# When two weight loads and four transposing loads may start, in a one-core forward and backward pass of an attention and feed-forward block

## The chip, the cores and the metric

The kernel runs on one core of one Trainium2 chip. The metric is the time of one execution on the device in microseconds (us), and lower is better. A core has TensorE (PE in the profile) for matrix products, VectorE (DVE), ScalarE (ACT) and GpSimd (POOL) for the rest, and SyncE (SP), which here only issues transfers. POOL issues transfers too, through a queue of its own, and a few come from ACT. An engine works through its own list of instructions strictly in the order in which the program lists them: an instruction that has to wait holds back all that stand behind it on that engine, transfers to be issued included.

## The reference, cut to what matters

The reference returns the output of a block and the gradients of seven inputs for a given `grad_out`. Sequence length is 2048, width 512, 32 heads of 16, feed-forward width 1792, all bf16.

```
def _A_ref(x, wqkv, wo):            # attention over 8 positions back, in steps of 2
    q, k, v = split(x @ wqkv)
    logits = einsum(q, k gathered at pos - 2*w, w = 0..7) * scale
    attn = softmax(logits)
    return einsum(attn, v gathered) @ wo
def _B_ref(x, w1, b1, w2, b2):
    return gelu(x @ w1 + b1) @ w2 + b2
h  = x + _A_ref(layernorm(x), wqkv, wo)
h2 = h + _B_ref(layernorm(h), w1, b1, w2, b2)
```

`jax.vjp` of `h2` gives the gradients of x, wqkv, wo, w1, b1, w2 and b2.

## The kernel before, in words

The 2048 tokens are worked in four chunks of 512 (`c` = 0 to 3). The forward pass has these steps for each chunk, each a function.

- `f_ln1` and `f_qkv` (lines 348 to 377): layer norm, the projection to q, k or v, and the writing of the result to a buffer in DRAM (`q_r`, `k_r`, `v_r`) with four transfers.
- `f_attn` (line 417): products of q and k on DVE (`pa`), their sums over a head on PE (`lg`), the softmax, whose `Exp` on ACT is line 436, and the writing of the weights to `at_r` by four POOL transfers (line 442). The mark `("e", c, i)` is set on the `Exp` of half `i` of chunk `c`.
- `f_o` (line 444): the weights are read back by SP (`a`, line 300), v is read by SP in four parts (`v`, line 282), DVE multiplies the two (`pbo`, line 330, eight instructions per chunk), PE sums (`pso`), and ACT copies the result to `otm` (line 451). The mark `("o", c, qd)` is set on the copy of part `qd`. The result is written to DRAM by POOL (line 452) and transposed on PE and ACT to `oT`.
- `f_h` (line 457): product with `wo` on PE (`psh`, line 463), residual on DVE (line 464), the second layer norm (statistics on DVE at lines 259 to 261, a power on POOL at line 263, its application at line 265), writing to DRAM by POOL (line 467), transposing to `ln2T`.
- `f_ffn1` (line 497): first feed-forward product with `w1` on PE (`psf`, line 506), gelu on ACT and DVE, and three POOL transfers for each of seven steps (`x_d`, `s_d`, `g_d`, line 526).
- `f_ffn2` (line 529): product with `w2` (line 535).

Lines 553 to 634 write these calls out in an order that mixes the chunks. That order is not the order on the engines: the framework's scheduler lists each engine's instructions by priority and by the time at which it reckons them ready. So a transfer that is written early but depends on something late can stand behind others in the queue. `gate(ins, key)` (line 111) makes an instruction depend on the one that set a mark.

`w1` and `w2` are loads of 1792 KB each, both issued by POOL (lines 584 and 587). Their buffers are shared with earlier data: `w1` takes over `early1` (x of chunks 1 and 2 and a transposed layer norm), `w2` takes over `early` (k and q of chunk 1, read by the `pa` products of `f_attn(1)`). `w1` is first read by `f_ffn1(0)`, `w2` by `f_ffn2(0)`.

The backward pass ends with three weighted sums per chunk (`b_sum(c, sel)`, line 847). For `sel` 1, the last of the three, each of four parts is two DVE products (`pb`), a PE sum (`pss`) and an ACT copy (line 863) into `gt`. The mark `("s", c, sel)` is overwritten by each part, so after the call it stands for the fourth. Then `b_gx` (line 878) needs the three results of a chunk transposed (`gT`), multiplies them with `wqkvT` on PE (`psy`, line 892) and goes through the backward layer norm (`ln_bwd`, line 643). For chunks 0 and 1 all transposing is done by PE. For chunks 2 and 3 `b_gT` (line 868) has POOL write the results of `sel` 2 and 0 to DRAM (`gq_d`, line 875) and SP load them back transposed (`gTo`, line 876); `sel` 1 is transposed by PE. All four transposing loads are gated on `("s", 3, 1)`. For chunks 2 and 3 `psy` takes the operands in the order `sel` 1, 2, 0. Products for the gradient of wqkv (`psq`, line 929) are mixed in between.

## Time and profile before

| | |
|---|---|
| median of 6 runs | 714.42 us |
| lowest to highest | 712.17 to 720.34 us |
| the profiled execution: its time | 712.17 us |
| its span, first to last instruction | 709.9 us |
| mean granted TensorE clock | 0.955 |
| PE busy | 623.0 us (88%) |
| DVE busy | 556.5 us (78%) |
| ACT busy | 395.3 us (56%) |
| transfers | 163.57 MB, mean 230 GB/s |

The profiled execution is one of the six. It stands 2.25 us below their median, and 2.27 us of its time lie outside the span. In a timeline a line gives the start and the length of a group of instructions, the engine, the line of the kernel, the operation with output and inputs, and in brackets how long the engine was idle before it and what ended that. POOLq and SPq are the queues in which POOL and SP issue transfers; a line there shows the issuing, not the landing. In a table by stretches (windows) each engine's busy time is followed by the number of its instructions, then come the granted TensorE clock as a share of full speed, the mean busy share of the 16 DMA engines, and what they moved in GB/s.

### The profile page before, as it was taken

What the parts mean: (1) busy time and instruction counts of PE and PEld (TensorE: products, weight loads), DVE (VectorE), ACT (ScalarE), POOL (GpSimd) and SP (SyncE); (2) the same over time, 40 slices, a digit from 0 to 9 for tenths busy, and PEclk for the clock granted to TensorE, in tenths of its full rate; (3) what the DMA queues carried; (4) which work ended last, traced back from release to release, by engine and by line L of the source; (5) the groups of instructions that cost most, each with busy time, mean ns of one, the idle gap of its engine ahead of it and who ended that gap; (6) DMA issues with size and microseconds to landing.
All of it is one profiled execution on the core that took longest, in us unless ns stands there. A gap on an engine that the chain in (4) does not pass through costs nothing. (4 is left out here: it accounts for less than half of the span.)

```text
span 709.9 us, 10264 instructions
## 1 busy us (share of the span) xinstructions
PE 623.0 (88%) x3614; PEld 264.6 (37%) x3682; DVE 556.5 (78%) x919; ACT 395.3 (56%) x548; POOL 210.0 (30%) x318
## 2 busy tenths in 40 slices
PE   1898668779789499999999999998999999999985
PEld 0333222234243134444444444443533333334432
DVE  6467958778973859975988788477899999999754
ACT  5654425877957739845867687552131135357543
POOL 4324323534533433452452433313200410001000
PEclk9999887969989789999999999999999999999999
DMA  8597798664789659666775985849799999986642
GB/s 236 149 270 224 197 372 277 233 254 155 253 296 232 222 156 209 200 200 256 198 213 103 182 210 142 256 117 245 287 355 378 312 340 302 347 294 202 172 105 67
DMA packets 103221, 163.57 MB, mean 230 GB/s; under 512 B 60961, under 2 KB 69250, under 8 KB 103170
## 3 DMA queue, kind: packets, MB, share of 16 engines
q1 hardware_dynamic: 73824, 78.40, 40.4%
q0 software_dynamic: 24720, 80.07, 34.7%
q10 hardware_dynamic: 4626, 4.46, 1.9%
q8 instruction: 28, 0.46, 0.3%
q14 instruction: 23, 0.19, 0.1%
HBM read 90.97 MB, written 56.71 MB: 208 GB/s over the span
## 5 line engine op out<-in xcount | busy, mean ns | idle before, releaser
L330 DVE TENSOR_TENSOR pb<-ba,r 128x2048 bf16<-128x2048 bf16 x96 | 111.5, 1220 | 0.6 <-PE ptq L274 0.3
L506 PE MATMUL psf<-ln2T,w 128*128 128x512 bf16 x218 | 57.7, 396 | 12.6 <-ACT u L508 11.9
L535 PE MATMUL ps<-w,g 128*128 128x512 bf16 x216 | 55.2, 379 | 0.3
L788 PE MATMUL psw<-h1tm,ln2a 128*128 128x512 bf16 (+1 forms) x249 | 53.4, 353 | 0.5 <-issue 0.3
L667 PE MATMUL psw<-gout,gtm 128*128 128x512 bf16 x202 | 50.4, 379 | 2.8 <-DMA gtm<-g_d 1.5
L719 PE MATMUL psx<-w1T,gh 128*128 128x512 bf16 x211 | 49.8, 379 | 0.3
L330 DVE TENSOR_TENSOR pbo<-a,v 128x2048 bf16<-128x2048 bf16 x32 | 38.2, 1218 | 14.1 <-DMA a<-at_r 9.6
L372 ACT CAST qkv<-psq 128x512 bf16<-128x512 f32 x48 | 27.6, 585 | 32.2 <-PE psq L370 32.0
L697 PE MATMUL psg<-goutT,w2T 128*128 128x512 bf16 x161 | 41.2, 379 | 0.4
L508 ACT ACTIVATE u<-psf,b1c 128x512 bf16<-128x512 f32 x56 | 36.0, 681 | 7.9 <-PE psf L506 4.8
L506 PEld LDWEIGHTS <-w 128*128 128x128 bf16 x224 | 20.9, 100 | 41.5 <-issue 24.0
L518 ACT ACTIVATE s<-z 128x1024 bf16<-128x1024 bf16 x28 | 29.6, 1059 | 11.5 <-DVE z L516 7.2
L710 POOL DMA_DIRECT2D h1tm_d<-th x27 | 20.6, 762 | 50.2 <-ACT th L708 36.3
L313 DVE TENSOR_TENSOR pag<-go,bv 128x2048 bf16<-128x2048 bf16 x24 | 28.6, 1220 | 8.5 <-DMA go<-go_r 4.4
L863 ACT ACTIVATE gt<-pss 128x512 bf16<-128x512 f32 x32 | 19.1, 597 | 28.5 <-PE pss L336 28.5
L708 ACT COPY th<-pth 128x1024 bf16<-128x1024 bf16 x27 | 27.0, 1000 | 11.5 <-PE pth L706 10.9
L788 PEld LDWEIGHTS <-ln2a 128*128 128x128 bf16 x256 | 22.6, 98 | 27.7 <-issue 10.2
L689 ACT ACTIVATE by<-bu 128x1024 bf16<-128x1024 bf16 x21 | 22.2, 1057 | 19.2 <-DVE gb1p L699 16.4
L892 PE MATMUL psy<-wqkvT,gT 128*128 128x512 bf16 x121 | 30.9, 379 | 0.7 <-DVE lua L653 0.2
L929 PE MATMUL psq<-gt,ln1a 128*128 128x512 bf16 x123 | 31.1, 380 | 0.3 <-issue 0.2
L526 POOL DMA_DIRECT2D g_d<-g x28 | 20.6, 734 | 36.3 <-DVE g L520 34.5
L336 PE MATMUL pss<-pb,sel 128*32 128x512 bf16 x384 | 29.5, 384 | 0.6 <-DVE pb L330 0.2
(221 smaller groups left out, 1361.1 us busy)
## 6 DMA issues: line engine op xcount, KB each, us to landing
v<-v_r SPq DMA_DIRECT2D x16, 576.0 KB, 6.9
r<-go_r SPq DMA_DIRECT2D x16, 576.0 KB, 7.6
r<-k_r SPq DMA_DIRECT2D x16, 576.0 KB, 6.9
r<-q_r SPq DMA_DIRECT2D x16, 576.0 KB, 5.6
g_d<-g POOLq DMA_DIRECT2D x28, 256.0 KB, 4.2
h1tm_d<-th POOLq DMA_DIRECT2D x27, 256.0 KB, 4.5
h1tm<-h1tm_d POOLq DMA_DIRECT2D x3, 2048.0 KB, 12.1
x_d<-u POOLq DMA_DIRECT2D x21, 256.0 KB, 5.5
```

The source lines that it names most:

```text
L330: last = nc.vector.tensor_tensor(out=pr[:], in0=_ap(a_ap, [a_ap.ap[0], [2 * H, CJ], [0, Q4], [1, H]], off=wh * H + (4 * H * wh if sg else 0)),
L336: mm = nc.tensor.matmul(ps[PR * n:PR * n + PR, :], lhsT=sel4[:], rhs=prs[wh][:, TC * n:TC * n + TC, :, :].rearrange("p j d h -> p (j d h)" ...
L506: nc.tensor.matmul(ps[:], lhsT=w1[0][:, dc, ft * P:(ft + 1) * P], rhs=ln2T[:, dc, :], start=(dc == 0), stop=(dc == DC - 1))
L508: nc.scalar.activation(out=u[:, i, :], in_=ps[:], func=ACT.Identity, bias=b1c[:, ft:ft + 1], scale=1.0)
L518: nc.scalar.activation(out=s[:], in_=z[:], func=ACT.Sigmoid, scale=2.0 * GC)
L535: nc.tensor.matmul(ps[:], lhsT=gs[ft // 2][:, ft % 2, j * P:(j + 1) * P], rhs=w2[0][:, ft, :], start=(ft == 0), stop=False)
L667: nc.tensor.matmul(ps[:], lhsT=gtm[:, t, :], rhs=gout[t // TC][:, t % TC, :], start=(t == 0), stop=(t == NT - 1))
L697: nc.tensor.matmul(ps[:], lhsT=w2T[:, dc, ft * P:(ft + 1) * P], rhs=gT[:, dc, :], start=(dc == 0), stop=(dc == DC - 1))
L719: nc.tensor.matmul(ps[:], lhsT=t1s[ft // 2][:, ft % 2, j * P:(j + 1) * P], rhs=w1T[:, ft, :], start=(ft == 0), stop=(ft == FT - 1))
L788: nc.tensor.matmul(ps[:, 0:nf * P], lhsT=ln2a[:, t // TC, t % TC, dc * P:(dc + 1) * P], rhs=tmx[:, t, 0:nf * P], start=(t == 0), stop=(t = ...
L892: nc.tensor.matmul(ps[:], lhsT=gT[sel][:, g, j * P:(j + 1) * P], rhs=wqkvT[:, sel * G + g, :], start=(n == 0), stop=(n == NJ - 1))
L929: nc.tensor.matmul(ps[:], lhsT=ln1a[t // TC][:, t % TC, dc * P:(dc + 1) * P], rhs=gts[sel, t // TC][:, t % TC, :], start=(t == 0), stop=(t ...
```

## The change

Three things are edited, and no instruction is added or taken out.

1. The load of `w1` is written right after `f_attn(1)` instead of after `f_o(0)`, and it waits for the `Exp` of the first half of chunk 1 instead of the first `otm` copy of chunk 0.
2. The load of `w2` is written after `f_o(1)`, behind `f_qkv(2, 2)` and `f_ffn1(0)`, instead of after `f_h(0)`. It waits for the first `otm` copy of chunk 1 instead of the `Exp` of the first half of chunk 1. The wait for its buffer (the `pa` products of chunk 1) is there in both.
3. Each part of `b_sum` also gets a mark of its own for `sel` 0 and 1. The two transposing loads of chunk 2 are gated on the first part of the last sum (`("s", 3, 1, 0)`), the two of chunk 3 on its third part (`("s", 3, 1, 2)`); before, all four waited for its fourth.

```
     f_attn(1)
+    w1.append(fl.tile([P, DC, F], BF16, name="w1", tag="w1", bufs=1))
+    gate(pq.dma_start(out=w1[0][:], in_=B_w1.rearrange("(dc p) f -> p dc f", p=P)), ("e", 1, 0))
     f_o(0)
-    w1.append(fl.tile([P, DC, F], BF16, name="w1", tag="w1", bufs=1))
-    gate(pq.dma_start(out=w1[0][:], in_=B_w1.rearrange("(dc p) f -> p dc f", p=P)), ("o", 0, 0))
     f_h(0)
-    w2.append(fb.tile([P, FT, D], BF16, name="w2", tag="w2", bufs=1))
-    gate(pq.dma_start(out=w2[0][:], in_=B_w2.rearrange("(ft p) d -> p ft d", p=P)), ("e", 1, 0))
     f_qkv(2, 2)
     mix(f_ffn1(0), none)
     f_o(1)
+    w2.append(fb.tile([P, FT, D], BF16, name="w2", tag="w2", bufs=1))
+    gate(pq.dma_start(out=w2[0][:], in_=B_w2.rearrange("(ft p) d -> p ft d", p=P)), ("o", 1, 0))
     f_h(1)
...
-                mark["s", c, sel] = nc.scalar.activation(out=o_ap, in_=i_ap, func=ACT.Copy, scale=scale)
+                mark["s", c, sel] = mark["s", c, sel, qd] = nc.scalar.activation(out=o_ap, in_=i_ap, func=ACT.Copy, scale=scale)
...
-            gate(sync.dma_start_transpose(out=gTs[sel, c], in_=d_t[:, :]), ("s", 3, 1))
+            gate(sync.dma_start_transpose(out=gTs[sel, c], in_=d_t[:, :]), ("s", 3, 1, 2 * (c - 2)))
```

## The prediction

> **What bounds the kernel now.** I read the page's busy shares and slices first, then the table by stretches around the two weight loads, then the timelines of POOL, SP and DVE there, and last the timelines of the end.

> ```profile
> PE 623.0 (88%) x3614; PEld 264.6 (37%) x3682; DVE 556.5 (78%) x919; ACT 395.3 (56%) x548; POOL 210.0 (30%) x318
> ...
> PE   1898668779789499999999999998999999999985
> ```

> PE is nearly full in the backward pass (slices of 17.7 us, from the 15th on) and has its holes in the forward pass. So a stall of PE in the backward pass costs its own length, and a forward wait costs what it delays the chain between DVE, PE and ACT. The loads of w1 and w2 lie in the sixth slice:

> ```profile
> 80.00:90.00 10.00, 6.82 (x54) 2.62 (x52) 9.86 (x11) 6.30 (x11) 4.72 (x8) 0.98 0.74 204
> 90.00:100.00 10.00, 8.69 (x38) 3.06 (x37) 5.17 (x11) 1.60 (x2) 2.78 (x5) 0.68 1.03 352
> 100.00:110.00 10.00, 3.85 (x23) 1.04 (x21) 6.11 (x11) 2.83 (x5) 2.69 (x4) 0.83 1.02 412
> 110.00:120.00 10.00, 8.68 (x46) 3.59 (x43) 7.25 (x9) 5.26 (x7) 2.81 (x5) 0.66 0.65 210
> ```

> From 90 to 110 us the DMA engines are full (1.03, 1.02), while PE is busy for only 3.85 us of the second ten. POOL's queue, then SP's, then DVE:

> ```profile
> 85.28 2.17 POOL L179 DMA_DIRECT2D at_r<-attn  x4 [10.77 <-DVE attn L440]
> 87.44 1.13 POOL L587 DMA_DIRECT2D w<-in_B_w_dram  x1
> ...
> 93.46 0.76 POOL L584 DMA_DIRECT2D w<-in_B_w_dram  x1
> ```

> ```profile
> 70.12 2.39 SPq L300 DMA_DIRECT2D a<-at_r  x4
> ...
> 93.75 4.53 SPq L300 DMA_DIRECT2D a<-at_r  x4
> 98.33 1.89 SPq L282 DMA_DIRECT2D v<-v_r  x3
> ```

> ```profile
> 100.50 0.17 DVE L260 BATCH_NORM_AGGREGATE mvb<-stb 128x2 f32<-128x6 f32 x1
> 104.21 1.23 DVE L330 TENSOR_TENSOR pbo<-a,v 128x2048 bf16<-128x2048 bf16 x1 [3.54 <-DMA a<-at_r]
> 105.35 0.17 DVE L260 BATCH_NORM_AGGREGATE mvb<-stb 128x2 f32<-128x6 f32 x1
> 105.44 1.19 DVE L330 TENSOR_TENSOR pbo<-a,v 128x2048 bf16<-128x2048 bf16 x1
> 106.55 0.16 DVE L261 TENSOR_SCALAR veb<-mvb 128x4 f32<-128x4 f32 x1
> 107.06 2.36 DVE L330 TENSOR_TENSOR pbo<-a,v 128x2048 bf16<-128x2048 bf16 x2 [0.35 <-DMA v<-v_r]
> 109.34 1.38 DVE L265 TENSOR_SCALAR ln<-h,mvb,rstd 128x512 bf16<-128x512 bf16 x4
> ```

> The weights of chunk 1 are written at 85.28 and w2 (3.5 MB with w1) starts right behind them. SP can read them back only from 93.75, its four issues take 4.53 us where those of chunk 0 took 2.39, and DVE stands still for 3.54 us. Behind that pbo, in DVE's order, is the layer norm of chunk 0, for which the first psf at 114.47 waits. At the other end:

> ```profile
> 668.28 4.94 SPq L876 DMA_TRANSPOSE gTo<-gq_d  x2
> ```

> ```profile
> 674.07 1.03 PE L892 MATMUL psy<-wqkvT,gTo 128*128 128x512 bf16 x4
> 677.15 1.04 PE L892 MATMUL psy<-wqkvT,gTo 128*128 128x512 bf16 x4 [2.05 <-DMA gTo<-gq_d]
> ```

> The copy that opens the gate ends at 668.26 and the first transposing load starts at 668.28: the gate is the last wait. PE, otherwise full here, loses 2.05 us.

> **The change part by part.** Nothing is added; three waits move. I take each against the profiled execution (712.17 us, span 709.9).

> w1 goes earlier. Its new gate, the Exp at 72.89, ends at 73.5; POOL is then issuing the v writes until 74.5 and afterwards idle until 85.28 (10.77 us). So the issue (0.76 to 1.13 us) costs POOL nothing, and what is behind it in that queue, the at_r writes, comes 10 us later. The load landed in 11.6 and 15.4 us beside the other, so from 75 it is there by about 90, against a first use at 114.47. Its buffer is free: the last psq product on it ends by 66.4. From 78.4 to 81.7 nothing moves at all, so there is room. It can only hurt the weights of chunk 0, issued 70.12 to 72.5 and used at 78.56. Their landing has a median of 4.9 us and a maximum of 6.9; with the maximum they come at 79.4, 0.85 late. Bounds 0 and +0.85; I take +0.2, since they mostly land before w1 moves.

> w2 goes later. Its gate, the copy at 107.83, moves forward with the rest to about 104. I expect the issue after POOL's power for the layer norm (106.80 now), because the veb that releases that power precedes the copy (106.55 and 107.83). Were it ahead, the power would wait for the copy's end (108.41 now) and for an issue of 1.13 us: 108.41 + 1.13 - 106.80 = 2.7 us more; the bounds are 0 and +2.7, and I take 0. Behind it in POOL's queue are v writes and the ln2 write, read by nothing until later chunks, and then the x_d writes from 118.81; u has three buffers, and an x_d write that lands at the page's median of 5.5 us instead of the 3.3 measured there would hold the fourth u back by at most 2.2. I take 0, as 111 to 118 are nearly idle for DMA. w2 is first used at 155.36, so 13.5 us from 108 leaves over 30 us to spare.

> What goes: the at_r writes end at 87.45. For chunk 0 SP started 3.47 us after their end (66.65 to 70.12); so 90.9, four issues 2.39, the last landing 4.9 after its start, 97.6. That is 3 us before DVE gets to the pbo at 100.67. The v loads follow at 93.3 and land 6.6 later, at 99.9 to 101.2, before they are used. Both waits go: 3.54 + 0.35 = 3.89. They cannot give more, because DVE is then in its own work, and the 4.67 us of idle before 95.33 wait for psh, a chain of pso, copy, transpose and product without a transfer. What is late next is PE: its v projection ends at 103.03 and pso can follow at once.

> The clock. PE stands still 3.66 us before 106.69, and from 108 to 116 the granted clock is 0.50. The 15 transposes ptb took 0.93 + 1.01 where 8 take 0.61 elsewhere, 0.75 more; seven psf took 1.49 + 1.21 where seven take 1.69 at 118.81, 1.0 more. So between 0 and 1.75 us come on top; I take 1.0, since the clock was also low (0.68) from 90 to 100, where no gap of PE exceeds 1 us. [...]

> [...]

> The transposing loads. Chunk 2's new gate is the copy at 656.18; its writes to gq_d, issued at 654.70 and 655.45, land in 4.6 and 5.4 us, at 660.9. Two loads take 4.94 us to issue and land 5.2 to 6.6 after their start, so by about 670; the first use is at 674.07. Chunk 3's gate opens at 664.6; its loads follow, are issued by 670.4, and are needed from about 682. In SP's queue the gx writes of chunk 1, ready at 670.7, are behind them; the last r load (651.90) is ahead. The stretch 663 to 668 has no transfers at all. The 2.05 us go (bounds 0 and 2.26, with the 0.21 at 681.64); behind them PE finds all operands, and the ring of two psy buffers moves up with it.

> Sum: -3.89 - 1.0 + 0.2 - 2.05 = -6.74 us, that is 705.4 in an execution like the profiled one. That one lies 2.25 below the median, so 714.42 - 6.74 = 707.7.

> **The rivals.**
> 1. The forward gain is given back before 260 us. For it: later holes, such as DVE's 6.03 us for the weights of chunk 3 at 229.72 and ACT's 2.40 for an s_d write at 147.46. Against it: these follow from work before them and move with it. Only the end gains: 712.4.
> 2. Only the forward part gains, because the loads at the end start early but land late among the gq_d writes: 714.42 - 4.69 = 709.7. Against it: 4 us of slack.
> 3. Nothing changes, each wait being replaced by one of its length: 714.4.
> 4. Slower: w2 sits in POOL's queue behind the stores of f_ffn1(0), since it is now written behind them. First use 155.36, less 4.7 gained, is 150.7; the landing takes 13.5. Break-even is a landing 6.7 late, at 157.4, so an issue at 143.9, or 148.6 on the clock before: behind the s_d store at 148.81 or a later one it decides. Behind the last g_d store (157.0, less 4.7, is 152.3) it lands at 165.8, 15.1 late; 707.7 + 15.1 = 722.8. Against it: POOL's order follows readiness (w2 went ahead of w1, and the otm write of chunk 1 stands at 138.41 among the f_ffn1(0) stores).
> 5. More: the clock term in full, and a reordering that shortens a later hole by as much as the 3.5 us of this one: 703.4.

> **How the numbers follow.** Forecast 0.50, with a range of its own from 705 to 711 (the clock term whole or absent, the +2.7); rival 1 0.20, rival 2 0.06, rival 3 0.06, rival 4 0.12, rival 5 0.06. The range 703 to 717 takes in all but rival 4 and the tail of rival 5. One per cent, about what can be told from no change, is 7.1 us: faster means below 707.3. Rival 5 and half of the forecast (its range is cut about in the middle there) lie below it: 0.31 for faster. The other half and rivals 1 to 3 make 0.57 for the same, and rival 4 makes 0.12 for slower.

> **What would show it.** Right: w1 issued near 75 and w2 after 104 in POOL's queue; no idle on the weights of chunk 1 before pbo; first psf near 110; the transposing loads starting near 661; no PE wait on gTo. Wrong: w2 after 143 with the first product on it waiting; a new DVE wait before 79; the layer norm's power held behind w2; the first psf early but the backward pass starting no sooner.

## The result, and the profile after

The changed kernel took 709.29 us (median of 16 runs, 703.25 to 712.62) against 716.09 us for the kernel before (median of 37 runs, 711.18 to 720.34). The ratio is 0.9906, with a 95% interval from 0.9882 to 0.9929: 6.7 us less, and between 5.1 and 8.4. The forecast was 6.74 less.

The two profiled executions do not show this difference. That of before took 712.17 us, one of the shortest of its 37; that of after took 711.75, one of the longest of its 16. Their spans, 709.9 and 709.7, differ by 0.2. So what follows reads stretches and waits from the traces, and totals from the medians.

Busy time and PE's slices on the page of after are nearly those of before, as they must be when only waits move:

```profile
PE 623.3 (88%) x3614; PEld 264.8 (37%) x3682; DVE 555.7 (78%) x919; ACT 395.1 (56%) x548; POOL 210.2 (30%) x318
...
PE   1898668779698499899999999998999999999995
```

The table by stretches of after, same columns as before:

```profile
80.00:90.00 10.00, 7.63 (x46) 2.86 (x44) 9.02 (x11) 5.51 (x10) 2.97 (x6) 0.91 0.58 149
90.00:100.00 10.00, 7.59 (x43) 2.83 (x45) 5.76 (x10) 2.79 (x4) 3.94 (x7) 0.83 1.01 343
100.00:110.00 10.00, 4.79 (x30) 1.50 (x28) 7.60 (x15) 2.83 (x5) 4.62 (x6) 0.96 0.97 332
110.00:120.00 10.00, 8.68 (x43) 3.57 (x44) 7.55 (x9) 6.08 (x8) 2.95 (x4) 0.70 0.94 297
```

From 90 to 110 us the transfer engines are still full (1.01, 0.97); w2 now fills the next ten (0.94, 0.65 before). POOL's timeline tells why:

```profile
86.96 2.17 POOL L179 DMA_DIRECT2D at_r<-attn  x4 [13.00 <-DVE attn L440]
89.19 0.78 POOL L583 DMA_DIRECT2D w<-in_B_w_dram  x1
...
106.66 1.93 POOL L263 TENSOR_TENSOR rstd<-veb,half 128x4 f32<-128x4 f32 x1 [0.80 <-DVE veb L261]
...
111.67 1.12 POOL L590 DMA_DIRECT2D w<-in_B_w_dram  x1
```

Line 583 is w1 and line 590 is w2. w2 went where it was forecast, behind the power. w1 did not go ahead of the at_r writes, 10 us earlier: POOL idles for 13.00 us and then writes at_r, and w1 stands directly behind, in the place that w2 had. So one of the two loads has left the full stretch, not both. SP in after still starts reading late and takes 4.78 us for the four issues (4.53 before, 2.40 for chunk 0 in this trace):

```profile
95.85 4.78 SPq L300 DMA_DIRECT2D a<-at_r  x4
100.68 1.89 SPq L282 DMA_DIRECT2D v<-v_r  x3
```

and DVE still waits for the weights, 2.40 instead of 3.54 us, though no longer for v:

```profile
104.07 1.23 DVE L330 TENSOR_TENSOR pbo<-a,v 128x2048 bf16<-128x2048 bf16 x1 [2.40 <-DMA a<-at_r]
...
105.30 1.19 DVE L330 TENSOR_TENSOR pbo<-a,v 128x2048 bf16<-128x2048 bf16 x1
...
106.48 2.35 DVE L330 TENSOR_TENSOR pbo<-a,v 128x2048 bf16<-128x2048 bf16 x2
108.76 1.45 DVE L265 TENSOR_SCALAR ln<-h,mvb,rstd 128x512 bf16<-128x512 bf16 x4
```

At the end the change does what was said. SP starts the transposing loads 7.4 us sooner, all four in one go:

```profile
660.88 12.05 SPq L876 DMA_TRANSPOSE gTo<-gq_d  x4
```

and PE's timeline has no wait for them, where 2.05 us stood before:

```profile
113.72 1.49 PE L506 MATMUL psf<-ln2T,w 128*128 128x512 bf16 x3 [0.22 <-issue]
...
676.16 1.89 PE L892 MATMUL psy<-wqkvT,gTo 128*128 128x512 bf16 x8
```

The first psf comes at 113.72, only 0.75 earlier than before, because the at_r writes of this execution began 1.68 later. Counted from the at_r writes it is 26.76 us against 29.19.

### The profile page after: what moved, and what is told of

Same layout as the page of the kernel before. It is cut to its first block, busy times and chain, and to the rows that moved or that the text cites. A ratio compares the mean times of both kernels' runs of the same rounds, so it can differ in the third digit from the quotient of the medians.

```text
span 709.7 us, 10265 instructions
## 1 busy us (share of the span) xinstructions
PE 623.3 (88%) x3614; PEld 264.8 (37%) x3682; DVE 555.7 (78%) x919; ACT 395.1 (56%) x548; POOL 210.2 (30%) x318
## 5 line engine op out<-in xcount | busy, mean ns | idle before, releaser
L330 DVE TENSOR_TENSOR pb<-ba,r 128x2048 bf16<-128x2048 bf16 x96 | 111.5, 1216 | 0.7 <-DMA r<-go_r 0.5
L330 DVE TENSOR_TENSOR pbo<-a,v 128x2048 bf16<-128x2048 bf16 x32 | 38.2, 1216 | 12.5 <-DMA a<-at_r 8.8
L708 ACT COPY th<-pth 128x1024 bf16<-128x1024 bf16 x27 | 27.0, 999 | 11.5 <-PE pth L706 11.5
L689 ACT ACTIVATE by<-bu 128x1024 bf16<-128x1024 bf16 x21 | 22.2, 1057 | 18.8 <-DVE gb1p L699 16.5
L892 PE MATMUL psy<-wqkvT,gT 128*128 128x512 bf16 x122 | 31.1, 379 | 0.8 <-DVE lua L653 0.2
L667 PEld LDWEIGHTS <-gtm 128*128 128x128 bf16 x208 | 19.6, 99 | 28.4 <-issue 5.3
```

The costliest lines, as they stand in the source:

```text
L330: last = nc.vector.tensor_tensor(out=pr[:], in0=_ap(a_ap, [a_ap.ap[0], [2 * H, CJ], [0, Q4], [1, H]], off=wh * H + (4 * H * wh if sg else 0)),
L667: nc.tensor.matmul(ps[:], lhsT=gtm[:, t, :], rhs=gout[t // TC][:, t % TC, :], start=(t == 0), stop=(t == NT - 1))
L892: nc.tensor.matmul(ps[:], lhsT=gT[sel][:, g, j * P:(j + 1) * P], rhs=wqkvT[:, sel * G + g, :], start=(n == 0), stop=(n == NJ - 1))
```

## The experiments

The theory at this point: the gain has two halves, the waits for the weights of chunk 1 in the forward pass and the PE wait on `gTo` at the end, and they add. Its rivals: only one half pays; one weight load alone pays; or the places in the queues, not the gates, decide. Differences are medians against the kernel before on the same chip, as the ratio gives them, with the 95% interval; all times in us.

| run | median (runs) | before (runs) | ratio, 95% | difference |
|---|---|---|---|---|
| e1_tail: third edit only | 713.63 (6) | 716.60 (11) | 0.9962, 0.9926 to 0.9998 | -2.7 |
| e2_w1: first edit only | 715.20 (6) | the same | 0.9984, 0.9942 to 1.0026 | -1.1 |
| e3_w2: second edit only | 715.26 (6) | the same | 0.9989, 0.9953 to 1.0026 | -0.8 |
| e4_weights: first and second | 713.08 (6) | the same | 0.9962, 0.9931 to 0.9993 | -2.7 |
| e5_w1_front | 713.41 (12) | 712.87 (29) | 1.0002, 0.9979 to 1.0025 | +0.1 |
| e6_w2_late | 728.37 (6) | the same | 1.0213, 1.0162 to 1.0264 | +15.2 |
| e7_w2_tail: second and third | 708.81 (12) | the same | 0.9920, 0.9889 to 0.9951 | -5.7 |
| e8_after_again: the changed kernel | 708.03 (12) | the same | 0.9922, 0.9893 to 0.9950 | -5.6 |
| e9_w1_act | 707.71 (7) | 713.78 (14) | 0.9905, 0.9869 to 0.9941 | -6.8 |
| e10_w1_split | 708.69 (8) | the same | 0.9923, 0.9894 to 0.9951 | -5.5 |
| e11_w1_h | 708.52 (6) | the same | 0.9913, 0.9882 to 0.9945 | -6.2 |
| e12_before_again | 713.82 (one run) | - | - | - |

Since whole executions differ by several us in places that the change does not touch, I also compare two stages in all traces. The forward stage runs from DVE's last softmax product of chunk 1 (line 440) to its first residual of chunk 1 (line 464). The end stage lies between two pieces of work of `ln_bwd` on DVE (line 648), from one in the last part of chunk 1 to the second of chunk 2.

| stage | without the edits to it | with all of them |
|---|---|---|
| forward (first and second edit) | before 67.3, e1 66.7, e12 65.0: mean 66.3 | after 65.1, e4 64.8, e8 63.9: mean 64.6 |
| its first part, from POOL's at_r writes to the first psf | before 29.2, e1 27.9, e12 27.2: mean 28.1 | after 26.8, e4 26.8, e8 26.1: mean 26.5 |
| end (third edit) | before 14.7, e12 15.4, e2 16.4, e3 16.0, e4 16.4: mean 15.8 | 12.5 in each of after, e1, e5 to e11 |

The traces with only one of the two weight edits are left out of the first two rows; there the forward stage is 67.8 in e2, 66.5 in e3 and 65.9 in e7. Two traces of the same program lie up to 2.3 us apart in it (before and e12), so a difference of 1.7 between two means of three is a rough figure.

**e1, the end alone.** The first two edits are undone.

```
-            gate(sync.dma_start_transpose(out=gTs[sel, c], in_=d_t[:, :]), ("s", 3, 1))
+            gate(sync.dma_start_transpose(out=gTs[sel, c], in_=d_t[:, :]), ("s", 3, 1, 2 * (c - 2)))
```

> Only the third edit (the transposing loads gated part by part); the weight loads as before. Theory A (the forecast's own terms): the loads start near 661, the wait of PE on gTo of 2.05 us goes, 2.0 us less than the kernel before. Rival B (the gain at the end is given back by products that PE then does after the last psy): 0 to 0.5 us less. Rival C (the whole 6.7 us come from here, the weight loads giving nothing): 6.7 us less.

Measured: 2.7 us less (0.1 to 5.3). SP's timeline of e1 shows the early start, and PE's (first line of the second fence) products without a wait:

```profile
659.68 11.79 SPq L876 DMA_TRANSPOSE gTo<-gq_d  x4
```

```profile
675.19 1.89 PE L892 MATMUL psy<-wqkvT,gTo 128*128 128x512 bf16 x8
```

The end stage falls from 15.8 to 12.5. The stage behind it, some products for the gradient of wqkv among it, grows from 19.3 to 19.8, so 0.5 is given back: 3.3 - 0.5 = 2.8. Rival 2, in which the end brings nothing, falls: by the times only just, but the stage is shorter in every trace with the edit than in every trace without it.

**e2, e3, e4: the weight loads one at a time and together.** The loads as in the change, with the third edit undone; e2 has the first edit, e3 the second, e4 both.

```
 e2:     f_attn(1)
+    gate(pq.dma_start(out=w1[0][:], ...), ("e", 1, 0))
     f_o(0)
-    gate(pq.dma_start(out=w1[0][:], ...), ("o", 0, 0))
 e3:     f_h(0)
-    gate(pq.dma_start(out=w2[0][:], ...), ("e", 1, 0))
...
     f_o(1)
+    gate(pq.dma_start(out=w2[0][:], ...), ("o", 1, 0))
```

> Only the first edit. In POOL's queue w1 now stands where w2 stood, right behind the at_r writes of chunk 1, and w2 comes where w1 was, so both loads still lie between 87 and 110 us. Theory A (what counts is how much of the two loads lies in that stretch): same as before within 1 us, and DVE still waits about 3.5 us for the weights of chunk 1. Rival B (an earlier w1 lets the feed-forward start sooner): 2 us or more less, and the first psf earlier with that wait unchanged.

> Only the second edit: w2 is issued after the ln2 write near 111, w1 stays behind its gate near 93, so that nothing large is issued right behind the at_r writes. Theory A: the at_r writes land by 91, the wait for the weights of chunk 1 goes wholly (3.5 us) and the time is 3.5 to 5 us less than before, that is more than with both weight edits. Rival B: w1 alone fills the stretch as well, the wait is 2 to 3 us and the gain 1 us.

> The first two edits without the third. Theory A: w1 right behind the at_r writes leaves about 2.4 us of the 3.5 us wait, as in the changed kernel; with shorter landings of v the stage gains about 2.2 us, so 2.2 us less than before. Rival B (the parts add up to the whole 6.7 us measured, so the end gives 2.0 and this 4.7): 4.7 us less.

Measured: -1.1 and -0.8 us alone, neither told apart from nothing, and -2.7 together (0.5 to 4.9). In e2 the two loads have merely changed places behind the at_r writes (w1 at 89.59, w2 at 95.82), and DVE's wait is even longer in its trace:

```profile
106.76 1.22 DVE L330 TENSOR_TENSOR pbo<-a,v 128x2048 bf16<-128x2048 bf16 x1 [4.70 <-DMA a<-at_r]
```

So w1's new gate by itself frees nothing in this trace. In e3 the wait for the weights did not go wholly, as theory A had it: 1.80 us of it is left and 1.22 for v, 3.02 together, as much as two other traces show with both loads in their old places (3.00 and 3.03, see e12). In e4 2.66 us are left, about what its theory A named. The e4 trace shows something else, at the end, where its old gates still hold. First its stretches, then PE's timeline:

```profile
676.00:678.00 2.00, 0.48 (x3) 0.00 (x0) 0.00 (x0) 0.00 (x0) 0.00 (x0) 1.00 1.13 342
678.00:680.00 2.00, 1.07 (x4) 0.51 (x5) 0.00 (x0) 0.00 (x0) 0.00 (x0) 0.84 1.08 115
680.00:682.00 2.00, 2.00 (x7) 0.64 (x5) 0.76 (x3) 0.69 (x2) 0.00 (x0) 0.50 1.04 236
682.00:684.00 2.00, 2.00 (x14) 0.98 (x13) 0.92 (x2) 0.96 (x2) 0.00 (x0) 0.81 0.99 188
```

```profile
678.93 1.51 PE L892 MATMUL psy<-wqkvT,gTo 128*128 128x512 bf16 x4 [2.45 <-DMA gTo<-gq_d]
...
681.10 2.72 PE L892 MATMUL psy<-wqkvT,gTo 128*128 128x512 bf16 x8
```

PE waits 2.45 us for the transposed operands, and then the granted clock falls to 0.50: four products take 1.51 where they took 1.04 in the trace of before, eight take 2.72 where they take 1.89 at full clock. The clock also fell to 0.50 behind this wait in e2 and e3, and stayed at 1.00 in before and e12. The profile that I forecast from was thus one of the cheap cases of this wait, which is in part why the stage without the edit has a mean of 15.8 and not 14.7.

**e5, w1 really early, through POOL's queue.** The changed kernel, with a higher priority for w1.

```
-    gate(pq.dma_start(out=w1[0][:], ...), ("e", 1, 0))
+    with tc.high_priority(120): gate(pq.dma_start(out=w1[0][:], ...), ("e", 1, 0))
```

> The changed kernel with w1 in the place in POOL's queue that the forecast had assumed, ahead of the at_r writes of chunk 1 (it stands behind the q writes and ahead of the wo loads, and goes out at about 73.5 us when its gate opens). Theory A (what is left of DVE's wait for the weights of chunk 1, 2.4 us, is w1 right behind the at_r writes): that wait goes, the layer norm of chunk 0 and the first psf come 2 to 2.5 us sooner counted from the end of the softmax of chunk 1, and the time is 2 us less than the changed kernel's. Rival B (a forward gain is given back at the wait for the weights of chunk 3 near 229 us): the same 2 us up to 200 us, and less than 1 us of it left at 313 and in the time. Rival C (w1 and what waits behind it now collide with the weights of chunk 0): a new wait of DVE before 79 us and no gain or a loss.

Measured: +0.1 us against before (-1.5 to +1.8), and 5.4 above e8 on the same chip. POOL's timeline of e5:

```profile
75.06 0.77 POOL L583 DMA_DIRECT2D w<-in_B_w_dram  x1 [5.78 <-ACT e L436]
75.82 2.79 POOL L241 DMA_DIRECT2D wo<-in_A_wo_dram  x4
...
84.81 0.55 POOL L179 DMA_DIRECT2D v_r<-qkv  x1 [4.53 <-DMA w<-in_B_w_dram]
86.53 0.55 POOL L179 DMA_DIRECT2D v_r<-qkv  x1 [1.18 <-DMA wo<-in_A_wo_dram]
```

w1 now stands ahead of the wo loads and the v writes. POOL is held 5.78 us by the gate, and further on 4.53 us until w1 has landed, before it issues the third v write. ACT then lacks a free copy buffer for 5.71 us. The profile names a k write as the last landing; the delayed v writes land at about the same time, and which of the two held the buffer is not shown. PE waits 5.78 us for that copy, DVE 7.15 for PE, and the first residual of chunk 0 comes 17.1 us after the softmax product, where it is 10.6 or 11.0 elsewhere. In return the wait for the weights is gone in DVE's timeline:

```profile
107.69 0.17 DVE L260 BATCH_NORM_AGGREGATE mvb<-stb 128x2 f32<-128x6 f32 x1
107.77 1.19 DVE L330 TENSOR_TENSOR pbo<-a,v 128x2048 bf16<-128x2048 bf16 x1
```

This does not show that the earlier issue removes the wait. DVE comes to this product at 107.77, later than in after (104.07), and SP starts to read the weights only at 99.28: the last of them lands at 104.62, 17.5 us after the first at_r write, against 17.0 in after. What e5 shows is the price in POOL's queue, 6.1 to 6.5 us through what is behind the load.

**e6, w2 too late.** The changed kernel, with w2 moved on, to see whether rival 4 has its price right.

```
     f_h(1)
     f_attn(2)
+    gate(pq.dma_start(out=w2[0][:], ...), ("e", 2, 1))
```

> The changed kernel with w2 written after f_attn(2) and gated on the Exp of its second half (near 161 us), so that it lands near 175, some 20 us after the first product on it in the changed kernel (near 152). It puts a price on a load that comes too late, the forecast's slower rival. Theory A (PE stands still for what it lacks): 10 to 15 us more than the changed kernel. Rival B (the scheduler puts other products of PE there, as it knows the gate): 0 to 3 us more.

Measured: 15.2 us above before (11.5 to 18.8) and 20.3 above e8. POOL issues w2 behind the stores of the feed-forward step, and PE's first product with w2 follows its landing:

```profile
162.17 1.13 POOL L592 DMA_DIRECT2D w<-in_B_w_dram  x1 [0.16 <-issue]
```

```profile
172.33 3.18 PE L535 MATMUL ps<-w,g 128*128 128x512 bf16 x14
```

That product starts at 154.66 in after and 152.67 in e8, so it is 17.7 to 19.7 late, and the total is 20.3 up, more than the 10 to 15 of theory A: here the load cost its lateness in full.

**e7, the changed kernel without its first edit.** w1 is where it was before; w2 and the end are changed.

> The second and third edits without the first: w1 goes out behind its old gate near 96, after the q writes, and w2 near 112. Theory A (the parts add up, and the second edit alone has given 0.8 us): 3.5 us less than before, 3 us more than the changed kernel. Rival B (it is enough that one of the two loads leaves the full stretch): the same as the changed kernel within 1 us.

Measured: 5.7 us less than before, e8 5.6. The first edit is thus not shown to matter. In e7 w1 is issued at 92.27 and w2 at 108.40: here too one load has left the stretch, and it is the same one. That is rival B. DVE waits 0.33 us for the weights and 1.10 for v in its trace.

**e8, the changed kernel again.** No edit.

> The changed kernel once more, beside the others on one chip. Theory A: 6.7 us less than before, within 1.7. In its profile the stage from the end of the softmax of chunk 1 (DVE line 440, fourth instruction) to the first residual of chunk 1 (line 464, fifth) is 2.2 us shorter than in the kernel before, and PE does not wait on gTo.

Measured: 5.6 us less (3.6 to 7.6), in agreement with the first measurement. PE does not wait on `gTo`, and DVE's wait for the weights is 0.99 us in this trace, where it was 2.40 in the first trace of the same program.

**e9, w1 early through ACT's queue.** The changed kernel, with ACT issuing w1 right behind the `Exp` that opens its gate.

```
-    gate(pq.dma_start(out=w1[0][:], ...), ("e", 1, 0))
+    gate(nc.scalar.dma_start(out=w1[0][:], ...), ("e", 1, 0))
```

> The changed kernel with w1 issued by ACT, in whose list it stands right behind the Exp that opens its gate (near 74 us), so that no other transfer waits behind it in POOL's queue. This is the place and time that the forecast had assumed, without the blocked writes of the run before. Theory A (the forecast's forward term): DVE does not wait for the weights of chunk 1, from the end of the softmax of chunk 1 to the first residual of chunk 1 it takes 2 to 2.4 us less than in the changed kernel, and the time is 2 us below the changed kernel's. Rival B (the layer norm and the products behind it are bound by something else there): the wait is gone and the stage is at most 1 us shorter. Rival C (the weights of chunk 0 or the v writes suffer as before): DVE waits more before 95 us, and the time is no better or worse.

Measured: 6.8 us less than before (4.2 to 9.4), not told apart from the changed kernel. This is the state that the forecast described: w1 is issued at 72.02 (ACT's timeline), and in DVE's timeline the weights are there when DVE gets to them: the last lands at 96.51, 12.9 us after the first at_r write, against 17.0 in after. The trace is of the fastest of the seven runs (701.59 us), so its stages may flatter the version.

```profile
72.02 0.41 ACTq L583 DMA_DIRECT2D w<-in_B_w_dram  x1
```

```profile
98.63 0.17 DVE L260 BATCH_NORM_AGGREGATE mvb<-stb 128x2 f32<-128x6 f32 x1
98.71 1.19 DVE L330 TENSOR_TENSOR pbo<-a,v 128x2048 bf16<-128x2048 bf16 x1
...
101.09 2.35 DVE L330 TENSOR_TENSOR pbo<-a,v 128x2048 bf16<-128x2048 bf16 x2
104.38 1.38 DVE L265 TENSOR_SCALAR ln<-h,mvb,rstd 128x512 bf16<-128x512 bf16 x4 [0.93 <-POOL rstd L263]
```

The next thing late is POOL's power: 0.93 us of new wait. The clock did not stay up either; the stretches of e9 around its first psf (108.44):

```profile
104.00:106.00 2.00, 1.22 (x9) 0.59 (x9) 1.62 (x5) 0.55 (x1) 1.56 (x3) 0.84 0.86 246
106.00:108.00 2.00, 0.90 (x9) 0.74 (x8) 2.00 (x3) 1.05 (x2) 1.89 (x3) 0.50 0.76 240
108.00:110.00 2.00, 2.00 (x11) 0.90 (x8) 2.00 (x3) 1.01 (x1) 0.34 (x1) 0.50 0.78 215
```

From the at_r writes to the first psf it takes 24.8 us, 1.7 less than the mean with both edits (26.5) and 3.3 less than without (28.1). The whole forward stage is 63.3, where those means are 64.6 and 66.3.

**e10 and e11, w1 in other places.** In e10 w1 comes in two halves of its columns, the second gated on the fourth `otm` copy of chunk 0. In e11 it waits for the first residual of chunk 0.

```
 e10:
-    gate(pq.dma_start(out=w1[0][:], ...), ("e", 1, 0))
+    gate(pq.dma_start(out=w1[0][:, :, 0:F // 2], ...), ("e", 1, 0))
     f_o(0)
+    gate(pq.dma_start(out=w1[0][:, :, F // 2:F], ...), ("o", 0, 3))
 e11:
+            mark["h", c, j] = nc.vector.tensor_tensor(out=h[:, j, :], in0=ps[:], in1=x[:, j, :], op=ALU.add)
...
     f_h(0)
+    gate(pq.dma_start(out=w1[0][:], ...), ("h", 0, 0))
```

> The changed kernel with w1 loaded in two halves of 896 columns, the first where w1 is now, the second behind the last otm copy of chunk 0. Theory A (the load right behind the at_r writes delays them and the reading of the weights in proportion to its size): the wait for the weights of chunk 1 is about half of 2.4 us and the time 1 us below the changed kernel's. Rival B: no difference, as the second half fills the stretch as well.

> The changed kernel with w1 gated on the first residual of chunk 0 (near 96 us) and written behind f_h(0), so that it goes out after the weights of chunk 1 have been asked for. Theory A: no wait for the weights of chunk 1; w1 lands near 108 to 110, before the first psf needs it; 2 us below the changed kernel. Rival B (w1 now lands after the first psf could start, and v of chunk 1 shares the stretch with it): the same as the changed kernel or up to 3 us more.

Measured: 5.5 and 6.2 us less than before, forward stages 65.1 and 65.0, as the changed kernel. In e11 the wait for the weights is gone, and one of 2.81 us for v has taken its place: w1 (issued at 98.03) now falls on the v loads instead. In e10 both waits are gone, and the first psf comes 24.4 us after the at_r writes, as early as in e9. But then ACT, with its buffer not yet free, waits for a store of the first feed-forward step:

```profile
140.64 1.06 ACT L518 ACTIVATE s<-z 128x1024 bf16<-128x1024 bf16 x1 [4.82 <-DMA s_d<-s]
```

At that place two waits of 0.95 and 2.40 stand in before, and one of 1.97 in e9. What e10 won by the psf is gone by the end of the stage. This is what rival 1 described, in one trace.

**e12, one more trace of the kernel before.**

> The kernel before once more, for a second profile. Theory A (the wait of PE on gTo varies from execution to execution, as in three runs that left the loads' gate alone, where the stretch from the last residual of chunk 1 to the second of chunk 2 at DVE line 648 was 16.0 to 16.4 us against 14.7 in the first profile): 15 to 16.5 us in that stretch, 12.5 with the new gate. Rival B: 14.7 again, so the other edits lengthen it.

Measured: 713.82 us in its one run. DVE's timeline:

```profile
104.36 1.23 DVE L330 TENSOR_TENSOR pbo<-a,v 128x2048 bf16<-128x2048 bf16 x1 [1.63 <-DMA a<-at_r]
...
108.24 2.36 DVE L330 TENSOR_TENSOR pbo<-a,v 128x2048 bf16<-128x2048 bf16 x2 [1.37 <-DMA v<-v_r]
```

The same program waits here for 1.63 + 1.37 = 3.00 us, where the trace I forecast from showed 3.89; e1, in which this part is also untouched, shows 2.17 + 0.86 = 3.03. The end stage took 15.4 us, within theory A, with the longest wait of all (2.76) and a full clock.

## Why the prediction was right, step by step

The difference held: 6.74 less was forecast, 6.7 and 5.6 were measured. The time itself was to be 707.7 and was 709.29, since the kernel before has a median of 716.09 over 37 runs and not the 714.42 of the first six. The terms held less well: the forward part was forecast too large and the end too small. That the difference came so close is luck.

- **w1 near 75 us, ahead of the at_r writes: wrong.** The gate permits it, but in POOL's list the load stands behind those writes, so it was issued at 89.19, though its gate was open from 74.4 (the end of that `Exp` in after). I had taken the opening of the gate for the place in the queue. Rival 4 was set aside with the same reasoning ("POOL's order follows readiness"), which for w2 happened to hold.
- **w2 behind the power, without harm: right.** It was issued at 111.67 and first read at 154.66. The slower rival did not occur, but e6 shows its price: with w2 issued at 162.17, the first product on it starts 17.7 to 19.7 us late and the time rises by 20.3.
- **Both DVE waits go, 3.89: too large.** In after 2.40 remain, and the wait before was itself a long sample: 3.00 and 3.03 in the two other traces of the same code. With both weight edits the wait is 2.40, 2.66, 0.99 and 0.66 (after, e4, e8, e6), 1.7 on average against 3.3 in the three without: about half of it went. The forward stage, clock included, fell by 1.7 (66.3 to 64.6); by the times of e4 it is 2.7 (0.5 to 4.9), where 4.69 was forecast. e9 removes the waits in full and gets 3.0 in that stage, e10 does so too and gets 1.2, each in one trace. So even with w1 where I had put it the term would rather have been 1 to 3.
- **The clock, 1.0: not seen in the products that were to gain it.** The term was my estimate, worked out from the rows of before and a PE gap that was to vanish, and no run shows it. The forecast priced 15 ptb and seven psf at half clock; in after they take 0.93 + 1.01 and 1.49 + 1.15 us, against 0.93 + 1.01 and 1.49 + 1.21 before, so 0.06 of the 1.75 went. The granted clock was still 0.50 from 110 to 114 and 0.52 from 114 to 116, and in e9, where the wait that I blamed is gone, 0.50 from 106 to 112. The low stretch did get shorter at its front: it lasts 10.2 us in before, e1, e2, e3, e7 and e11, and 6.8 in after, e4, e5, e6, e8, e9 and e10, but also in e12, the kernel before. In after eight pso ran at full clock by that (0.61 us instead of 1.05); what this was worth is not shown. PE has little to do there with or without that wait: in after no gap from 104 to 110 is longer than 2.15 us, but PE is busy for only 0.40 and 0.61 of two stretches of 2 us from 104 to 108, and the clock falls at 109.1.
- **Harm to the weights of chunk 0, 0.2: not tested,** as w1 never moved there in the changed kernel. e9 has it there, and DVE's timeline of e9 shows no wait for a transfer at that place.
- **The end, 2.05: right in mechanism, too small.** The 7.4 us earlier start, the absent wait and the wait's place all came as said. It is worth 2.8 by the stages and 2.7 (0.1 to 5.3) by the times, because the wait is 2.0 to 2.8 us over five traces and in three of them the clock falls to 0.50 behind it; later products gave 0.5 back. One reading was wrong without effect: 4.6 and 5.4 us are medians over the writes of both chunks, and the two writes of chunk 2 landed at 658.5 and 660.1 in before, not at 660.9.

The stages add up to 1.7 + 2.8 = 4.5, against 5.6 (3.6 to 7.6) and 6.7 (5.1 to 8.4) by the times; e1 and e4, also by the times, add up to 5.4. What makes the rest is not settled; single traces of one kernel differ by more than that in stages that no edit touches. It also stays open how the forward gain divides between the first two edits: e7 does without the first and loses nothing that can be seen, but e3, the second alone, shows only 0.8 (from 3.4 less to 1.9 more).

Of the rivals, 2 and 3 are excluded by the intervals of e1 and of after. Rival 1 (only the end gains) would be 2.7 or 2.8 in all, below both intervals of the changed kernel; e1's own interval reaches up to 5.3, but that of e4 (0.5 to 4.9) stands against a forward part of nothing. Rivals 4 (slower) and 5 (11.0 less) lie outside both intervals of the changed kernel. On how early these two loads should be issued the runs show bounds on both sides: w2 later by some 24 us, together with w1, gained 2.7 in e4; later by 75 it cost 20.3 in e6; and w1 earlier had a shorter stage through ACT's queue, in one trace, and lost 5.4 through POOL's.

No version beat the changed kernel by more than the intervals; e9 is the nearest to it, with 0.9905 against 0.9906 and 0.9922.

## What to carry to other kernels

In these runs a gate said from when a transfer might start (w1 in after: from 74.4 us); the place in the issuing engine's list said when it did (89.19), and whom it held up (POOL for 5.78 us in e5). Before a load is put earlier, read what is ahead of it and behind it in that list (e5 against e9). A wait in one trace is a sample (3.89, 3.00 and 3.03 us for the same code here): before it goes into a sum at full length, look for the same wait in more executions, and for whether the clock falls behind it (to 0.50 in e2, e3 and e4, not in before and e12).

## What the runs showed of the hardware that was not expected

```profile
101.75 2.59 POOL L263 TENSOR_TENSOR rstd<-veb,half 128x4 f32<-128x4 f32 x1
```

 In e5, e9 and e10 it came too late by that, and DVE waited for it for 0.93. So where DVE's transfer wait was gone, the next step on POOL was longer, and part of the gain went there. In these seven the power ends about 0.9 us after a pbo has ended: the first one in after, e4, e6 and e8, the second in e5, e9 and e10 (in e9 that one ends at 103.44 and the power at 104.34). It was seen in the fourteen traces; no run was made to test it by itself, and what links the two instructions is not shown.
- **POOL stopped issuing until an earlier load of its own had landed,** though what it was to issue does not use that load. In e5 a v write stood 4.53 us behind w1. Waits of 4.07 and 4.88 us that end with w1's landing are in after and e4 as well, ahead of the zeroing of a pad. What makes POOL wait there the traces do not show.
